# Another work order for a recurrent attention block: new TensorE orders and list priorities, masks and identity ahead of the first norm, W_O in sixteen loads

## The chip, the cores and the metric

The kernel runs on one core of one Trainium2 chip. The metric is the device time of one execution in microseconds (us). Before the change three runs gave 803.99, 806.18 and 807.5 us; the median is 806.18 us.

## The reference

```python
def _A_ref(x, mem0, Wq, Wk, Wv, Wo, seg_len):     # x 1 x 2048 x 512, 32 heads of 128, seg_len 32, M = 8
    mem = mem0
    for s in range(n_seg):                        # 64 segments
        xs = x[:, s * seg_len:(s + 1) * seg_len, :]
        h = jnp.concatenate([mem, xs], axis=1)    # 40 rows
        q, k, v = h Wq, h Wk, h Wv                # 512 -> 32 x 128 each
        scores = where(mask, q k^T * scale, -1e9)
        o = softmax(scores) v
        o = jnp.einsum('bhte,hed->btd', o, Wo)
        mem = o[:, :M, :]                         # the memory of the next segment
        outs.append(o[:, M:, :])
    return jnp.concatenate(outs, axis=1)

h = x + _A_ref(_layernorm(x), mem0, Wq, Wk, Wv, Wo, 32)
h2 = h + _B_ref(_layernorm(h), w1, b1, w2, b2)    # layernorm, 512 -> 1792, gelu, 1792 -> 512
```

What matters is the recurrence: the first eight output rows of a segment are the first eight input rows of the next one. All products are bf16 with sums in f32.

## The kernel before, in words

All of W_Q, W_K, W_V and W_O (4 MB each) are loaded once and stay on the chip. The segments then run one after the other. Of the 40 rows of a segment, 32 (8 of memory and the first 24 tokens) stand as columns in `hT`, and go through the Q, K and V passes (`passes`, lines 794 and 796; a *unit* is four to sixteen TensorE instructions, the smallest part that an order can name). The last 8 tokens of a segment influence no later segment. Those of four segments are put together in `hB` (one tile of 128 tokens) and their passes are *fill work*, called F0 and F1 in the orders: it is put where TensorE would otherwise wait for the recurrence. W_O of the gathered rows (`wo_B`, line 1112, reads `OTB`) is fill work of the fourth segment.

One segment on TensorE is: Q0, K0, Q1, K1 (two halves of the heads), the scores SC0 and SC1 (line 963), V0 and V1, PVA (line 1055, the 24 tokens of the segment before), PV0 and PV1 (lines 994 and 998, probabilities times values), WO (line 1083, eight units), SA (line 1025, scores of the tokens). Then the recurrence closes: VectorE transposes the product of WO (`TT`, line 1095) and adds its halves into the `hT` of the next segment (line 1089), and only then can the first pass of the next segment read it. Softmax runs on VectorE (maxima `nmc` 972, reciprocals `rsc` 979, products `PC` 982, transposes `PTC` 983) and ScalarE (exponentials `EC`, line 976). Copies of PSUM go to ScalarE or VectorE, as `either` decides (lines 814 and 815).

A Python class records every operation and sets the order of each engine before anything is built. TensorE's order is written by hand: `START` for the opening with segment 0, and one string of `ORDERS` for each *place*: a1 to a3 for the first segments, m0 to m3 for the four places of the repeating cycle (segments 4 to 59, 14 cycles), z60 to z63 for the last. In such a string `WO.0.2` means units 0 and 1 of WO. `TURNED` names the passes that run backward at a place, so that a pass can start on the weights that the one before left in the array (`matmul_kept`, line 547, a matmul without a weight load). `LOCK` and `LEAD` place extra weight loads that change nothing (line 794), so that a cycle has a whole number of blocks of 256 TensorE instructions. The other engines are list-scheduled: an operation is taken by its rank plus `BONUS[kind@place]`; `HOIST` lets a wait be taken by an earlier TensorE instruction.

The opening: GpSimd builds `maskA` (lines 689 and 690), `maskR` and `maskL` (661 to 687), then `OTB`'s own masks (884 and 887) and `ident` (656 and 657), and computes the inverse deviations of the first two tiles of x (`rst`, 736 and 737). VectorE clears `OT`, `ZC` and `KALL` (693 to 696), takes the statistics of those tiles (734 and 735) and normalizes them (`xn`, 738). TensorE transposes them (748). The weights are issued on the SyncE queue (708, then 719 to 722 for W_O in eight pieces of 512 KB), the first tiles of x, the first memory and the bias of the MLP on ScalarE's queue (`first`, 711). The tiles of x from the third on come later and are transposed by DMA (755). In the fourth place of a cycle the product of `wo_B` is copied and added (1118 and 1119), in the first place of the next cycle its halves are added (`oBn`, 1120), and in the second the tile is added to x (1130). After segment 63 the MLP closes the kernel.

## Time and profile before

| | |
|---|---|
| three runs | 803.99, 806.18, 807.5 us; median 806.18 us |
| the profiled execution | 803.95 us; its span 802.2 us |
| mean granted TensorE clock | 0.998 |
| busy: TensorE, VectorE, ScalarE, GpSimd | 97%, 75%, 70%, 11% of the span |
| moved in the first 50 us | 18.18 MB, mean 364 GB/s |

The page gives for each engine its busy time, for each group of instructions its count, mean duration and the idle time ahead of it, and names what ended that idle time. In answers with a time line each row has the start, the duration (of a row with x4: of the four together), the engine, the line and the tiles, and in brackets how long the engine had been idle and what released it. Matmuls overlap, so a row's duration reaches into the next row; what counts is the distance from start to start. The queues' rows are marked SPq and ACTq.

### The profile page before, as it was taken

How to read it: one execution, taken by the hardware profiler on the slowest of the kernel's cores; microseconds unless marked ns; L12 is line 12 of the kernel's file. 1: busy time of each engine (PE TensorE's matmuls, PEld its weight loads, DVE VectorE, ACT ScalarE, POOL GpSimd, SP SyncE). 2: the span in 40 equal slices, each digit the busy share in tenths (PEclk: the TensorE clock that was granted, in tenths of full speed). 3: DMA queues.
4: the chain of work that ended last, by engine and by line, in shares of the span. 5: the costliest groups of instructions: out<-in, count | busy, mean ns of one | idle time of the engine just before them, and what ended most of it. 6: DMA issues, size and time to landing. Idle time of an engine off the chain costs nothing.

```text
span 802.2 us, 46835 instructions
## 1 busy us (share of the span) xinstructions
PE 775.9 (97%) x21699; PEld 423.1 (53%) x20880; DVE 600.7 (75%) x1847; ACT 558.0 (70%) x1580; POOL 90.1 (11%) x211
## 2 busy tenths in 40 slices
PE   2899999999999999999999999999999999999998
PEld 1455555555555555555555555555555555644444
DVE  3277878888888888888888888888888888732311
ACT  1557777777777777777778777777777777773342
POOL 5022000010001010101010101000000000020700
PEclk9999999999999999999999999999999999999999
DMA  9961010201111121102010202010212112074300
GB/s 367 394 174 24 4 37 11 45 12 37 26 33 30 30 33 27 36 19 42 19 43 15 49 12 50 13 37 20 50 25 56 51 38 59 17 232 127 86 27 26
DMA packets 65555, 48.77 MB, mean 61 GB/s; under 512 B 28996, under 2 KB 63308, under 8 KB 63820
## 3 DMA queue, kind: packets, MB, share of 16 engines
q1 hardware_dynamic: 65024, 45.50, 20.3%
q8 instruction: 166, 2.72, 1.4%
q14 instruction: 33, 0.27, 0.1%
q10 hardware_dynamic: 332, 0.27, 0.1%
HBM read 31.08 MB, written 8.13 MB: 49 GB/s over the span
## 4 chain that ended last, share of the span: by engine, by line
PE 91%; DMA 3%; DVE 2%; ACT 1%; SPq 1%; issue 1%; POOL 0%; DVEq 0%; ACTq 0%
PE ps L796 43%; PE ps L1083 15%; PE ps L547 8%; PE quad L1465 6%; PE ps L1451 5%; DMA WQ<-in_A_Wq_dram 3%; PE ps L1112 3%; PE quad L994 3%; PE quad L1055 2%; PE ps L1025 2%; PE ps L1233 1%; PE ps L963 1%; PE quad L963 1%; SPq L708 1%; PE quad L998 1%
## 5 line engine op out<-in xcount | busy, mean ns | idle before, releaser
L1083 PE MATMUL ps<-WO,OT 128*32 128x256 bf16 x4224 | 140.6, 274 | 0.1
L796 PE MATMUL ps<-WQ,hT 128*32 128x512 bf16 x1864 | 131.6, 379 | 0.7 <-DVE hT L1089 0.5
L796 PE MATMUL ps<-WV,hT 128*32 128x512 bf16 x1364 | 125.2, 381 | 0.0
L796 PE MATMUL ps<-WK,hT 128*32 128x512 bf16 x1700 | 123.6, 380 | 0.1
L815 ACT ACTIVATE kq<-ps 128x512 bf16<-128x512 f32 x160 | 95.4, 597 | 32.3 <-PE ps L796 26.4
L1083 PEld LDWEIGHTS ps<-WO,OT 128*32 128x32 bf16 x4224 | 100.9, 96 | 26.5 <-ACT OT L814 5.5
L814 ACT CAST kq<-ps 128x512 bf16<-128x512 f32 x162 | 94.8, 585 | 19.9 <-PE ps L796 13.1
L814 ACT CAST OT<-quad 128x128 bf16<-128x128 f32 x191 | 84.4, 442 | 27.0 <-PE quad L998 18.8
L839 DVE STREAM_TRANSPOSE KALL<-kq 128x256 f32<-128x256 f32 x160 | 71.2, 445 | 15.0 <-ACT kq L814 11.8
L796 PEld LDWEIGHTS ps<-WQ,hT 128*32 128x32 bf16 x1864 | 50.3, 97 | 58.8 <-issue 19.0
L861 POOL COPY ZC<-QTB 128x256 bf16<-128x256 bf16 x64 | 25.6, 401 | 477.2 <-PE ps L963 455.7
L796 PEld LDWEIGHTS ps<-WK,hT 128*32 128x32 bf16 x1700 | 45.8, 96 | 56.9 <-issue 14.5
L547 PE MATMUL ps<-WV,hT 128*32 128x512 bf16 x684 | 67.6, 379 | 0.0
L796 PEld LDWEIGHTS ps<-WV,hT 128*32 128x32 bf16 x1364 | 38.4, 97 | 47.3 <-issue 36.6
L839 DVE STREAM_TRANSPOSE QT<-kq 128x256 f32<-128x256 f32 x128 | 57.0, 445 | 6.5 <-ACT kq L815 1.9
L1454 ACT ACTIVATE WQ<-ps,b1t 128x512 bf16<-128x512 f32 x42 | 28.9, 688 | 46.6 <-PE ps L1451 46.6
L1095 DVE STREAM_TRANSPOSE TT<-ps 128x256 f32<-128x256 f32 x66 | 29.7, 450 | 36.3 <-PE ps L1083 36.1
L814 ACT CAST VS<-ps 128x512 bf16<-128x512 f32 x65 | 38.1, 586 | 26.6 <-PE ps L796 26.5
L814 DVE CAST VS<-ps 128x512 bf16<-128x512 f32 x63 | 41.8, 663 | 5.4 <-PE ps L796 5.4
L1541 DVE TENSOR_TENSOR WV<-quad,WV 128x512 bf16<-128x512 f32 (+1 forms) x16 | 10.5, 672 | 45.6 <-PE quad L1465 45.6
L982 DVE TENSOR_TENSOR PC<-EC,rsc 128x128 bf16<-128x128 f32 x128 | 39.7, 310 | 4.3
L1112 PE MATMUL ps<-WO,OTB 128*32 128x512 bf16 x512 | 42.1, 381 | 0.4 <-issue 0.2
(163 smaller groups left out, 1432.1 us busy)
## 6 DMA issues: line engine op xcount, KB each, us to landing
WV<-in_A_Wv_dram SPq DMA_DIRECT2D x4, 1024.0 KB, 8.5
WK<-in_A_Wk_dram SPq DMA_DIRECT2D x4, 1024.0 KB, 14.2
WQ<-in_A_Wq_dram SPq DMA_DIRECT2D x4, 1024.0 KB, 24.7
WO<-in_A_Wo_dram SPq DMA_DIRECT2D x8, 512.0 KB, 9.4
v_last<-VSB SPq DMA_DIRECT2D x60, 64.0 KB, 2.9
VBD<-v_last SPq DMA_DIRECT2D x60, 64.0 KB, 2.9
h_mid<-xr SPq DMA_DIRECT2D x16, 128.0 KB, 1.8
WK<-in_B_w_dram SPq DMA_DIRECT2D x4, 512.0 KB, 4.6
```

Of the source, the lines that this page charges most:

```text
L547: return e.add_instruction(mybir.InstMatmult(name="I-%d" % (4000000 + _kept[0]), engine=mybir.EngineType.PE, start_tensor_calc=start, stop ...
L796: ins = e.matmul(o, l, m, start=(k == 0), stop=(k == DC - 1), tile_position=(0, 32 * j), skip_group_check=True)
L814: return {"act": (lambda e: e.copy(out, src), t_act(n, ps_)), "dve": (lambda e: e.tensor_copy(out, src), 0.16 + 1.042e-3 * n * fast)}
L815: return {"act": (lambda e: e.mul(out, src, scale_), t_act(n, ps_)), "dve": (lambda e: e.tensor_scalar(out, src, scale_, None, ALU.mult), ...
L839: S.op("dve", lambda e: e.transpose(out, src), reads=[("kq", i)], writes=[key], dur=t_dve(256) + 0.02, after=after)
L982: S.op("dve", lambda e: e.tensor_tensor(PC[:, r].rearrange("p t a -> p a t"), EC[:, r], bc, ALU.mult), reads=[("EC", r), ("rsc", r)], writ ...
L1083: ins = e.matmul(ps[bank][32 * j:32 * j + 32, 0:256], lhs(slot(h)), wo_cols(h, b), start=(k == 0), stop=(k == 15), tile_position=(0, 32 * ...
L1095: S.op("dve", lambda e: e.transpose(tt.rearrange("p c q t -> p (c q t)"), ps[bank][:, 0:256]), reads=[("ps", bank)], writes=[("TT", par)], ...
L1112: ins = e.matmul(ps[bank][32 * j:32 * j + 32, :], OTB[:, bk % 2, slot(h), :], WO[:, h, :], start=(k == 0), stop=(k == 7), tile_position=(0 ...
L1451: ins = e.matmul(ps[bank][:, 0:SBT], W1[:, cc, fc * P:(fc + 1) * P], hnT_of(k)[:, cc, :], start=(cc == 0), stop=(cc == DC - 1))
L1454: S.op("act", lambda e: e.activation(gT[:, fc, :], ps[bank][:, 0:SBT], ACTF.Gelu_apprx_tanh, bias=b1t[:, fc:fc + 1], scale=1.0), reads=[(" ...
L1465: S.op("pe", lambda e: e.matmul(quad[:, t, :], lhs, W2[:, fc, :], **flags), reads=[("W2", part_of(fc))] + gT_keys(k, fc), writes=[("ps", t ...
```

## The change

Nothing changes in what is computed. Four things change:

1. `BONUS`, the table of priorities, gets other numbers for all kinds and places; `TURNED`, `ORDERS`, `LOCK` (106 to 108) and `LEAD` (199 to 189) are replaced. `START`, the order of TensorE in the opening, is left as it is.
2. The priority of `ident` goes from -40 to 40, so that GpSimd builds it first, with the masks behind it.
3. The tiles 0 and 1 of x are issued first on ScalarE's queue, ahead of the memory `m0` and the bias `b1n`, and this order is fixed with `behind`.
4. W_O is loaded in 16 DMAs of two heads in place of 8 of four, and a unit of WO waits for the pieces that it reads.

```diff
-LOCK = 106
+LOCK = 108
...
-LATE, RAW, LEAD = 0, 12, 199
+LATE, RAW, LEAD = 0, 12, 189
...
-TURNED = {"a1": "K0 Q1 V0", "a2": "K0 Q0", "a3": "V1", "m0": "F0 F1 Q0 V0", "m1": "K0 K1 Q1 V0", ...
+TURNED = {"a1": "K1 Q0 Q1", "a2": "K0 K1 Q1 V0 V1", "a3": "Q0 V0", "m0": "F0 Q1 V0", "m1": "F0 K0 K1 Q1 V0", ...
...
-          "m3": "K0.0.1 Q0.0.2 ... SC1.0.1 F1.0.1 V1.3.4 PVA.0.2 PV0.0.1 F1.1.5 WO.0.1 PV1.0.1 WO.1.8 F1.5.7 SA.0.1 F1.7.8",
+          "m3": "K0.0.1 Q0.0.2 ... SC1.0.1 V1.3.4 F1.0.1 PVA.0.2 PV0.0.1 F1.1.4 WO.0.2 PV1.0.1 WO.2.8 F1.4.7 SA.0.1 F1.7.8",
...
         def first(fn, kb, writes):
-            S.dma(fn, kb, writes=writes, eng="act")
+            firsts.append(S.dma(fn, kb, writes=writes, eng="act", behind=firsts[-1] if firsts else None))
+        firsts = []
         load_x(0, first)
+        load_x(1, first)
         first(lambda e: e.dma_start(m0, A_mem0[0]), 8, ["m0"])
         first(lambda e: e.dma_start(b1n[:], b1_d), 4, ["b1n"])
-        load_x(1, first)
...
-        for g in range(4):
+        for q in range(8):
             for a in range(2):
-                h0 = 16 * (g // 2) + 8 * a + 4 * (g % 2)
-                load(lambda e, h0=h0: e.dma_start(WO[:, h0:h0 + 4, :], wo_d[:, h0:h0 + 4, :]), 590, [("WO", g, a)])
+                h0 = 16 * (q // 4) + 8 * a + 2 * (q % 4)
+                load(lambda e, h0=h0: e.dma_start(WO[:, h0:h0 + 2, :], wo_d[:, h0:h0 + 2, :]), 295, [("WO", q, a)])
...
-                S.op("pe", f, reads=[("WO", q // 2, a) for a in range(2)] + reads(q // 4), ...
+                S.op("pe", f, reads=[("WO", q, a) for a in range(2)] + reads(q // 4), ...
```

What stands where, at the three places of which the prediction speaks. From line 712 on, the lines of the changed kernel are one higher.

GpSimd in the opening, before. The two `rst` rows per tile of x end the norm's statistics:

```order
25 L666 AFFINE_SELECT maskL<-maskL 128x16
26 L884 MEMSET OTB 128x608
27 L887 AFFINE_SELECT OTB<-OTB 128x4x8 x4
28 L736 TENSOR_SCALAR rst<-agg 128x1
29 L737 TENSOR_TENSOR rst<-rst,cneg 128x1
30 L656 MEMSET ident 128x128
31 L657 AFFINE_SELECT ident<-ident 128x128
32 L736 TENSOR_SCALAR rst<-agg 128x1
33 L737 TENSOR_TENSOR rst<-rst,cneg 128x1
```

GpSimd at the same place of the changed kernel (`ident` is now at rows 6 and 9, ahead of all masks):

```order
27 L666 AFFINE_SELECT maskL<-maskL 128x16
28 L737 TENSOR_SCALAR rst<-agg 128x1
29 L738 TENSOR_TENSOR rst<-rst,cneg 128x1
30 L737 TENSOR_SCALAR rst<-agg 128x1
31 L738 TENSOR_TENSOR rst<-rst,cneg 128x1
32 L885 MEMSET OTB 128x608
33 L888 AFFINE_SELECT OTB<-OTB 128x4x8 x4
```

Both tiles' `rst` move ahead of the masks of `OTB`, and nothing of `ident` stands between them any more.

ScalarE later in the opening, in the softmax of segment 0, before (`EC` are the exponentials of the two halves in ps6 and ps7; `OT` takes the products PV0 and PV1; `maskAF` is put into a bank for SA):

```order
33 L976 ACTIVATE EC,smc<-ps6,nmc 128x64 x2
34 L976 ACTIVATE EC,smc<-ps7,nmc 128x64 x2
35 L815 ACTIVATE kq<-ps5 128x512
36 L814 CAST OT<-quad 128x4x4x8
37 L938 COPY ps5<-maskAF 128x256
38 L814 CAST OT<-quad 128x4x4x8
```

ScalarE at the same place of the changed kernel:

```order
32 L977 ACTIVATE EC,smc<-ps6,nmc 128x64 x2
33 L816 ACTIVATE kq<-ps5 128x512
34 L939 COPY ps5<-maskAF 128x256
35 L815 CAST OT<-quad 128x4x4x8
36 L977 ACTIVATE EC,smc<-ps7,nmc 128x64 x2
37 L815 CAST OT<-quad 128x4x4x8
```

The exponentials of the second half now stand behind a copy, a mask and the copy of PV0's product.

TensorE at the end of place m3, before (`WO,OTB` is the fill work, `WO,OT` the units of WO, `KALL,QT` is SA, `WQ,hT` the next segment's first pass):

```order
1221 L1112 MATMUL ps<-WO,OTB 32x512 x16
1222 L1083 MATMUL ps<-WO,OT 32x256 x8
1223 L994 MATMUL quad<-PTC,VS 128x16 x16
1224 L998 MATMUL quad<-PTC,VBD 128x64 x4
1225 L1083 MATMUL ps<-WO,OT 32x256 x56
1226 L1112 MATMUL ps<-WO,OTB 32x512 x8
1227 L1025 MATMUL ps<-KALL,QT 32x32 x32
1228 L1112 MATMUL ps<-WO,OTB 32x512 x4
1229 L796 MATMUL ps<-WQ,hT 32x512 x8
```

TensorE at the same place of the changed kernel:

```order
1265 L1113 MATMUL ps<-WO,OTB 32x512 x12
1266 L1084 MATMUL ps<-WO,OT 32x256 x16
1267 L995 MATMUL quad<-PTC,VS 128x16 x16
1268 L999 MATMUL quad<-PTC,VBD 128x64 x4
1269 L1084 MATMUL ps<-WO,OT 32x256 x48
1270 L1113 MATMUL ps<-WO,OTB 32x512 x12
1271 L1026 MATMUL ps<-KALL,QT 32x32 x32
1272 L1113 MATMUL ps<-WO,OTB 32x512 x4
1273 L797 MATMUL ps<-WQ,hT 32x512 x8
```

One unit of four matmuls of the fill work goes from ahead of WO to behind it.

VectorE at the end of place m0 in one of the 14 cycles, before:

```order
855 L1089 TENSOR_TENSOR opT<-TT 64x4x24 x2
856 L839 STREAM_TRANSPOSE KALL<-kq 128x256
857 L1120 TENSOR_TENSOR oBn<-OTB 32x512
858 L1095 STREAM_TRANSPOSE TT<-ps 128x256
859 L1089 TENSOR_TENSOR hT<-TT 64x4x8 x2
```

VectorE at the same place of the changed kernel:

```order
859 L1090 TENSOR_TENSOR opT<-TT 64x4x24 x2
860 L840 STREAM_TRANSPOSE KALL<-kq 128x256
861 L1121 TENSOR_TENSOR oBn<-OTB 32x512
862 L739 TENSOR_SCALAR xn<-xr,agg,rst 128x512
863 L1096 STREAM_TRANSPOSE TT<-ps 128x256
864 L1090 TENSOR_TENSOR hT<-TT 64x4x8 x2
```

The normalization of a later tile of x, which stood at the end of m3, has come between `oBn` and `TT`; it stands there in nine of the cycles.

## The prediction

> **What bounds the kernel now.** I read the page's totals first, then what ended the chain, then TensorE's waits.

> ```profile
> span 802.2 us, 46835 instructions
> PE 775.9 (97%) x21699; PEld 423.1 (53%) x20880; DVE 600.7 (75%) x1847; ACT 558.0 (70%) x1580; POOL 90.1 (11%) x211
> ...
> PE 91%; DMA 3%; DVE 2%; ACT 1%; SPq 1%; issue 1%; POOL 0%; DVEq 0%; ACTq 0%
> ```

> TensorE is busy for 97% of the span, and it is 91% of the chain that ended last. Its idle time is 802.2 - 775.9 = 26.3 us, and part of that is the opening, where nothing can run. A change of order that keeps all the work can win only from idle time or from a slower clock. So I looked up where TensorE waits, in the list of its waits (engine and line, what it waited for, total, times, longest).

> ```profile
> PE ps L924 <- POOL maskL L666: 9.3, 1, 9.3
> ...
> PE quad L748 <- DVE xn L738: 2.5, 1, 2.5
> ...
> PE ps L796 <- DMA WQ<-in_A_Wq_dram: 1.1, 1, 1.1
> ...
> PE ps L796 <- DVE hT L1089: 0.5, 2, 0.3
> ```

> The big waits are single ones, in the first 50 us. The wait on `hT`, the recurrence, is nearly absent: fill work covers it. The prediction therefore has two parts, the opening and the 14 cycles.

> **The opening: what the earlier norm is worth.** The first rows are GpSimd's and VectorE's, from the time line.

> ```profile
> 9.93 1.35 POOL L887 TENSOR_SCALAR_AFFINE_SELECT OTB<-OTB 128x32 bf16<-128x32 bf16 x4
> ...
> 12.57 0.29 POOL L657 TENSOR_SCALAR_AFFINE_SELECT ident<-ident 128x128 bf16<-128x128 bf16 x1
> ```

> ```profile
> 9.88 0.69 DVE L734 BATCH_NORM_STATS2 stt<-xr 128x6 f32<-128x512 bf16 x1 [6.82 <-DMA xr<-in_A_x_dram]
> ...
> 14.04 1.79 DVE L694 MEMSET KALL<- 128x2080 uint32 x1 [0.38 <-issue]
> ```

> The norm of tile 0 waits for the tile until 9.88, then on GpSimd for OTB's masks, which end at 11.28, and on VectorE `xn` stands behind a 1.79 us clear. In the changed kernel the tiles come first, the clears are done while the tile flies, and `rst` follows maskL directly. With `ident` (about half a microsecond) put ahead of masks that ended near 9.3, `rst` can run near 10 to 10.5 and TensorE can transpose near 11 to 12 in place of 16.04 (the first row below). What it does with that lead stands in TensorE's time line and in the chain.

> ```profile
> 16.04 0.61 PE L748 MATMUL quad<-ident,xn 128*128 128x128 bf16 x4 [2.50 <-DVE xn L738]
> 17.11 3.65 PE L796 MATMUL ps<-WV,hB 128*32 128x512 bf16 x32 [0.47 <-ACT hB L814]
> 20.51 2.61 PE L796 MATMUL ps<-WV,hT 128*32 128x512 bf16 x32
> ...
> 31.73 1.91 PE L796 MATMUL ps<-WK,hB 128*32 128x512 bf16 x32
> 33.47 0.82 PE L796 MATMUL ps<-WQ,hB 128*32 128x512 bf16 x12
> 35.34 0.40 PE L796 MATMUL ps<-WQ,hB 128*32 128x512 bf16 x4 [1.05 <-DMA WQ<-in_A_Wq_dram]
> ...
> 36.43 1.04 PE L796 MATMUL ps<-WQ,hB 128*32 128x512 bf16 x16
> 37.29 1.04 PE L796 MATMUL ps<-WQ,hT 128*32 128x512 bf16 x16
> 39.55 0.66 PE L963 MATMUL ps<-KALL,ZC 128*32 128x64 bf16 x32 [1.22 <-POOL ZC L861]
> ...
> 42.57 0.29 PE L994 MATMUL quad<-PTC,VS 32*128 32x16 bf16 x16 [0.44 <-ACT OT L814]
> ...
> 43.89 1.96 PE L796 MATMUL ps<-WQ,hB 128*32 128x512 bf16 x16
> ...
> 49.03 0.38 PE L796 MATMUL ps<-WQ,hT 128*32 128x512 bf16 x1
> ```

> ```profile
> 7.24 28.05 DMA WQ<-in_A_Wq_dram
> ```

> The chain goes through the last piece of W_Q, which lands at 7.24 + 28.05 = 35.29 us. The changed kernel moves the same bytes ahead of it, only the order of 260 KB changes. So TensorE still cannot finish the first Q pass before 35.3, however early it started. **The lead is worth nothing at its end**: the work from 17.11 to 33.47 ends some 3 us earlier (the first V pass must itself wait for W_V, so not the whole 4 to 5 us) and TensorE then waits some 5 us for W_Q in place of 1.05, with a unit here and there as the earlier pieces land. I take the gain at 0.

> **The opening: what it may cost.** The clock is the first cost. The table by stretches gives (busy times of PE, PEld, DVE, ACT and POOL, then the granted clock):

> ```profile
> 38.00:42.00 4.00, 1.98 (x76) 0.82 (x68) 2.40 (x9) 3.37 (x14) 1.14 (x3) 1.00 1.10 351
> 42.00:46.00 4.00, 3.56 (x113) 2.40 (x102) 1.98 (x6) 1.74 (x7) 0.00 (x0) 0.57 1.10 349
> ```

> A stretch that was half busy (1.98 of 4 us) is followed by one at a granted clock of 0.57, in which 16 matmuls took 1.96 us, against 1.04 at 36.43. The first V pass at 17.11, behind the long idle start, shows the same: 3.65 us for 32, against 1.91 at 31.73. In the changed kernel the new pause from about 30.5 to 35.3 is emptier than the stretch from 38 to 42, so I expect the three Q passes from 35.3 on (0.87 us each, start to start) to begin at half speed. In some 3.4 us, the length that fits the slow stretch of 42 to 46, half the work is done, a loss of 1.7 us. It reaches the scores, because SC at 39.55 waits for copies of these passes. Ends: 0, if the pause doesn't slow the clock, and 2.6, if all three passes run at half speed.

> [...]

> The second cost is ScalarE's new order. The rows before:

> ```profile
> 41.12 0.32 ACT L976 ACTIVATE EC<-ps,nmc 128x64 f32<-128x64 f32 x1
> ...
> 41.41 0.61 ACT L815 ACTIVATE kq<-ps 128x512 bf16<-128x512 f32 x1
> 42.19 0.27 ACT L814 CAST OT<-quad 128x128 bf16<-128x128 f32 x1 [0.16 <-PE quad L998]
> ```

> The last exponential started at 41.12 and PV1 followed at 42.57, 1.45 later. In the changed kernel the second half's exponentials wait behind the copy of PV0's product, which ends at 42.46, so the last one starts near 42.7 and PV1 near 44.2, 1.6 later. Some 0.3 of it comes back, since VectorE has less to do between. I take 1.3 (ends 0 and 1.6). Behind PV1 on TensorE stand SA and WO of segment 0, so it counts in full. [...] W_O in 16 pieces costs nothing that I can see: WO had no wait for a load, and the eight more issues lie on a queue that waits for the transfers anyway. Ends: 0 and 0.3. The opening in sum: 1.7 + 1.3 - 1.3 = **+1.7 us**, ends -1.3 and +4.5 (2.6 + 1.6 + 0.3).

> **The cycles: one more unit behind WO.** Rows at the end of an m2 and of the m3 behind it:

> ```profile
> 317.28 0.42 PE L1025 MATMUL ps<-KALL,QT 128*32 128x32 bf16 x32
> 317.53 1.06 PE L796 MATMUL ps<-WV,hB 128*32 128x512 bf16 x16
> 318.44 0.40 PE L796 MATMUL ps<-WK,hT 128*32 128x512 bf16 x4
> ...
> 327.70 0.60 PE L1112 MATMUL ps<-WO,OTB 128*32 128x512 bf16 x8
> ...
> 328.36 0.41 PE L1112 MATMUL ps<-WO,OTB 128*32 128x512 bf16 x4
> 328.86 1.26 PE L796 MATMUL ps<-WQ,hT 128*32 128x512 bf16 x20
> ```

> From the first fill behind WO to the first pass of the next segment it is 1.16 us at both (318.44 - 317.28, 328.86 - 327.70). This is the length of the recurrence, TT and the adds. In m2, SA and four units fill it. The 16 matmuls of the four take 0.91 (318.44 - 317.53), a unit of four 0.23. In m3 there are SA and three units, and the last one took 0.50 from start to start: 0.27 of waiting. The fourth unit behind WO, taken from ahead of it, uses this time. I take 0.20 a cycle, a little under a unit, 14 x 0.20 = **-2.8 us** (ends -3.8, all 0.27, and 0). The other places keep four units and SA behind WO in another order, all within 1.16: nothing.

> **The cycles: the norm between oBn and TT.** The same order stands once in the profile of before, and the other rows are the usual m0:

> ```profile
> 543.51 0.68 DVE L1120 TENSOR_TENSOR oBn<-OTB 32x512 bf16<-32x512 f32 x1
> 544.51 0.45 DVE L1095 STREAM_TRANSPOSE TT<-ps 128x256 f32<-128x256 f32 x1 [0.33 <-PE ps L1083]
> ```

> ```profile
> 584.68 0.68 DVE L1120 TENSOR_TENSOR oBn<-OTB 32x512 bf16<-32x512 f32 x1
> 585.46 0.41 DVE L1224 TENSOR_SCALAR xn<-xT,agg,rst 128x512 bf16<-128x512 bf16 x1
> 585.79 0.44 DVE L1095 STREAM_TRANSPOSE TT<-ps 128x256 f32<-128x256 f32 x1
> ```

> VectorE waits 0.33 us for WO ahead of TT. With the norm of 0.41 in it, TT starts 1.11 after oBn in place of 1.00, and the next segment starts later by as much: 9 x 0.10 = **+0.9 us** (ends 0 and 1.0). Kept matmuls and extra weight loads change in number, but weight loads overlap the matmuls and 16 units take the same step either way: 0, ends -0.8 and +0.8, because the pauses of TensorE that the list of waits doesn't explain may move.

> **The sum**: 1.7 - 2.8 + 0.9 = -0.2 us. Against the profiled execution that is 803.95 - 0.2 = 803.8; this execution lies 2.2 below the median of the runs shown, so against the median it is 806.18 - 0.2 = **806.0 us**. A measurement of this kernel can tell about 0.5%, 4.0 us: faster is under 802.1, slower over 810.2.

> **The rivals.** *The opening wins after all.* No slow clock behind the pause, none at 42 to 46 either, and PV1 hidden: -1.3 - 2.8 + 0.9 - 0.8 = -4.0, and without the norm's cost -4.9: 801.3 to 802.2, middle **801.8 us**. [...] Against it: the rows show PV1 bound by the exponentials.

> *The opening is cold.* All three Q passes at half speed, PV1 late by the whole 1.6, the slow stretch at WO as before, and only half of the m3 unit counts: 4.5 - 1.4 + 0.9 = +4.0, **810.2 us**, just at the bound; every further tenth makes it slower.

> *The recurrence gets longer* (this one ends slower). VectorE, 75% busy, has 0.33 us spare ahead of TT. If the new list puts more in front of it at other places (in m1 the add to x, line 1130, now stands directly ahead of TT, and copies of `ZC` go from ScalarE to VectorE), TT is late by 0.1 in each of the 56 segments: 5.6 in place of 0.9, so 1.7 - 2.8 + 5.6 = +4.5, **810.7 us**. It decides from 0.09 a segment on. Against it: VectorE also loses copies of `maskAF` to ScalarE at these places.

> *The change does nothing in the opening* and the cycles gain alone: -2.8 + 0.9 = -1.9, **804.3 us**.

> **How the numbers follow.** My forecast 806.0 has 0.40; the winning opening 0.25 (0.20 faster, 0.05 within); the cold opening 0.13 (0.09 slower, 0.04 within); the longer recurrence 0.14 (0.13 slower, 0.01 within); the neutral opening 0.08, all within 0.5%, of which it takes 0.05, with 0.03 for a slower case not named. Faster 0.20, within 0.55, slower 0.25. The range goes from 801.6, the winning opening, to 810.8, the longer recurrence.

> **What would show it.** In the changed profile: the transposes of tile 0 near 11 to 12 us; the wait for W_Q near 5 us ending at 35.3; a clock under 0.8 in the stretch behind it; PV1 over 1.5 us behind PV0; segment 1's first pass near 50.7 in place of 49.03; the last fill unit of m3 followed in 0.23 us; TT 1.11 behind oBn in nine cycles. I am wrong if W_Q lands earlier than 35, if the clock stays at 1.00 from 35 to 46, or if waits on `hT` appear in every segment.

## The result and the profile after

The changed kernel takes **810.01 us** (median of six runs, 809.52 to 810.27), and the kernel before 806.15 us in the runs beside it (six, 803.53 to 807.5). The ratio is 1.0058 with a 95% interval of 1.0038 to 1.0079: slower by 0.6%, 3.9 us. The forecast was 806.0. The profiled execution took 809.82 us with a span of 808.1 us, against 803.95 and 802.2 before; this pair differs by 5.9 us and not by 3.9, because the profiled execution of before is one of its faster ones. The accounts below are of the two profiled executions, so they have to add up to 5.9.

The page after, from the totals:

```profile
span 808.1 us, 46811 instructions
PE 778.0 (96%) x21683; PEld 421.0 (52%) x20865; DVE 589.9 (73%) x1849; ACT 558.4 (69%) x1578; POOL 87.4 (11%) x211
```

TensorE's idle time rose from 26.3 to 30.1 us, and its busy time by 2.1 us with the same work; its mean granted clock was 0.994 in this execution, against 0.998 before. The list of its waits (engine and line, what for, total, times, longest) has new rows:

```profile
PE ps L797 <- DMA WQ<-in_A_Wq_dram: 4.2, 2, 2.1
PE quad L995 <- DVE PTC L984: 2.8, 3, 2.2
...
PE ps L797 <- DMA WK<-in_A_Wk_dram: 1.0, 1, 1.0
PE ps L964 <- ACT ZC L854: 0.9, 1, 0.9
...
PE quad L1466 <- DVE WV L1542: 0.8, 2, 0.6
...
PE ps L1113 <- issue: 0.7, 2, 0.4
PE ps L797 <- DMA WV<-in_A_Wv_dram: 0.7, 1, 0.7
...
PE quad L749 <- DVE xn L739: 0.3, 1, 0.3
```

The wait for the norm fell from 2.5 to 0.3, as the change wants. The wait for W_Q rose from 1.1 to 4.2, and there are new waits for W_K and W_V (1.7 together), for the probabilities (PTC), for a copy of the queries (ZC), and in the MLP for a norm.

Where the 5.9 us lie is best read from the starts of TT, since one TT closes each segment. The two TT rows below are the last before and the last of the 14 cycles (segments 3 and 59), first of before, then after:

```profile
78.98 0.45 DVE L1095 STREAM_TRANSPOSE TT<-ps 128x256 f32<-128x256 f32 x1 [2.12 <-PE ps L1083]
...
657.92 0.45 DVE L1095 STREAM_TRANSPOSE TT<-ps 128x256 f32<-128x256 f32 x1 [2.16 <-PE ps L1083]
```

```profile
82.50 0.45 DVE L1096 STREAM_TRANSPOSE TT<-ps 128x256 f32<-128x256 f32 x1 [1.56 <-PE ps L1084]
...
662.57 0.45 DVE L1096 STREAM_TRANSPOSE TT<-ps 128x256 f32<-128x256 f32 x1 [1.96 <-PE ps L1084]
```

At segment 3 the changed kernel is 3.5 us late, at segment 59 4.65. The table has all parts, worked out from the starts of all TT rows and the ends of the spans:

| part | before | after | difference |
|---|---|---|---|
| start to TT of segment 0 | 47.97 | 51.96 | +4.0 |
| segments 1 to 3 | 31.01 | 30.54 | -0.5 |
| the 14 intervals that end with a TT of m0 | 144.94 | 149.63 | +4.7 |
| the same for m1 and m2 together | 287.22 | 287.26 | 0.0 |
| the same for m3 | 146.78 | 143.19 | -3.6 |
| segments 60 to 63 | 42.17 | 42.21 | 0.0 |
| TT of segment 63 to the end | 102.13 | 103.29 | +1.2 |

So there are three losses (the opening, m0 and the end) and one gain (m3).

**The opening.** TensorE's time line after; the rows of before that answer to these stand in the prediction:

```profile
10.76 0.61 PE L749 MATMUL quad<-ident,xn 128*128 128x128 bf16 x4 [0.33 <-DVE xn L739]
...
32.77 0.40 PE L797 MATMUL ps<-WQ,hB 128*32 128x512 bf16 x4 [2.09 <-DMA WQ<-in_A_Wq_dram]
35.30 0.62 PE L797 MATMUL ps<-WQ,hB 128*32 128x512 bf16 x4 [2.13 <-DMA WQ<-in_A_Wq_dram]
35.70 1.92 PE L797 MATMUL ps<-WQ,hT 128*32 128x512 bf16 x16
37.41 1.92 PE L797 MATMUL ps<-WQ,hB 128*32 128x512 bf16 x16
39.11 1.81 PE L797 MATMUL ps<-WQ,hT 128*32 128x512 bf16 x16
...
43.87 0.26 PE L995 MATMUL quad<-PTC,VS 32*128 32x16 bf16 x16 [0.26 <-DVE PTC L984]
...
46.33 0.26 PE L995 MATMUL quad<-PTC,VS 32*128 32x16 bf16 x16 [2.16 <-DVE PTC L984]
...
52.89 1.26 PE L797 MATMUL ps<-WQ,hT 128*32 128x512 bf16 x20
```

The norm is done 5.3 us earlier (10.76 against 16.04), W_Q lands at the same time (35.30 against 35.34), and what lies between is waiting. The Q passes then take 1.71 us from start to start in place of 0.87. PV1 comes 2.46 us behind PV0, where it was 0.76. The table by stretches (length, busy PE, PEld, DVE, ACT and POOL, then the granted clock, the DMA share and GB/s):

```profile
30.60:35.30 4.70, 0.47 (x9) 0.10 (x5) 0.45 (x1) 0.19 (x1) 0.00 (x0) 0.85 1.02 385
35.30:38.00 2.70, 2.70 (x28) 1.08 (x32) 0.45 (x1) 0.92 (x2) 0.00 (x0) 0.50 1.11 349
38.00:42.00 4.00, 3.23 (x48) 1.00 (x36) 1.97 (x5) 1.71 (x5) 0.74 (x2) 0.66 1.10 348
42.00:46.00 4.00, 1.48 (x52) 0.66 (x52) 2.08 (x9) 2.67 (x12) 0.40 (x1) 1.00 1.11 348
46.00:50.00 4.00, 3.67 (x112) 2.90 (x116) 2.57 (x8) 1.65 (x4) 0.00 (x0) 0.69 0.69 215
```

The clock was at half in the Q passes, as the prediction had it. Then came a second emptier stretch (1.48 of 4 us, the wait for PTC), and behind it a second slow one (0.69), in which W_O's units ran. The last term of the prediction's sum for the opening, -1.3 us, counted on the slow stretch of before (0.57 at 42 to 46) going away; a slow stretch was there all the same, 4 us later. The four runs below that keep this opening whole (4 to 7) have it too: clocks of 0.57, 0.65, 0.65 and 0.50 from 46 to 50 us.

**The cycles.** The end of m3 and the start of m0 in the same cycle, before and after. TensorE's rows:

```profile
286.42 0.86 PE L1112 MATMUL ps<-WO,OTB 128*32 128x512 bf16 x8
286.89 0.59 PE L1025 MATMUL ps<-KALL,QT 128*32 128x32 bf16 x32
287.31 0.41 PE L1112 MATMUL ps<-WO,OTB 128*32 128x512 bf16 x4
287.57 0.61 PE L796 MATMUL ps<-WQ,hT 128*32 128x512 bf16 x8
```

```profile
289.62 0.82 PE L1113 MATMUL ps<-WO,OTB 128*32 128x512 bf16 x11
290.84 0.38 PE L1113 MATMUL ps<-WO,OTB 128*32 128x512 bf16 x1 [0.40 <-issue]
...
291.25 0.41 PE L1113 MATMUL ps<-WO,OTB 128*32 128x512 bf16 x4
291.48 0.83 PE L797 MATMUL ps<-WQ,hT 128*32 128x512 bf16 x12
```

From the first fill to the next segment's first pass it was 1.15 us before, and is 1.86 now. In the changed kernel TensorE stops within a unit, between its 11th and 12th matmul, for 0.40 us and waits for nothing that the profile shows ("issue"). Before, a shorter stop of this kind lies in SA (0.42 from start to start, where 0.22 is usual), and costs nothing, since the recurrence needs 1.16 us anyway. With the fourth unit behind WO, no slack is left there. Over the 14 cycles the first pass after TT of m3 starts at the earliest 0.93 us behind it. Before, it is later than that in four cycles, by 0.7 us in all; as changed in ten, by 3.3 us.

The place is the end of a block of 256 instructions. This can be counted: take TensorE's records (matmuls, weight loads, waits) in order, and look for steps of more than 0.33 us from start to start within one unit, in segments 4 to 59. The 14 traces of this document (two here, twelve below) have 120 such steps, and the numbers of all 120 leave the same remainder when divided by 256.

So the 4.7 us of m0 have three parts. The stops before the first pass cost 2.6 us more than before (3.3 - 0.7). The norm ahead of TT costs 1.0, as the fifth run shows. The other 1.1 lie between the first pass and TT as well: 0.5 in the first m0, where TensorE waits for the probabilities, and some 0.05 in each of the others, and no run here shows their cause.

**The end.** SyncE's queue, first before, then after:

```profile
723.39 0.45 SPq L1178 DMA_DIRECT2D WQ<-h_mid  x1
...
724.37 2.68 SPq L1128 DMA_DIRECT2D oN<-oBn  x4
```

```profile
726.99 2.76 SPq L1129 DMA_DIRECT2D oN<-oBn  x3
729.92 0.35 SPq L1179 DMA_DIRECT2D WQ<-h_mid  x1
```

The second load of the MLP's input (`h_mid`) now stands behind three transfers of the last tile, and comes 6.5 us later (the segments are 4.7 us late by then). Its norm is what the MLP waits for in the list above (0.8 us).

### The profile page after: what moved, and what is told of

Same layout as the page of the kernel before. It is cut to its first block, busy times and chain, and to the rows that moved or that the text cites. A ratio compares the mean times of both kernels' runs of the same rounds, so it can differ in the third digit from the quotient of the medians.

```text
span 808.1 us, 46811 instructions
## 1 busy us (share of the span) xinstructions
PE 778.0 (96%) x21683; PEld 421.0 (52%) x20865; DVE 589.9 (73%) x1849; ACT 558.4 (69%) x1578; POOL 87.4 (11%) x211
## 4 chain that ended last, share of the span: by engine, by line
PE 90%; DMA 5%; SPq 2%; DVE 1%; issue 1%; ACT 0%; DVEq 0%
PE ps L797 43%; PE ps L1084 15%; PE ps L547 9%; PE quad L1466 4%; PE ps L1452 4%; PE ps L1113 4%; DMA WQ<-in_A_Wq_dram 3%; PE quad L995 3%; PE quad L1056 2%; PE ps L1026 2%; DMA WQ<-h_mid 1%; PE quad L964 1%; PE ps L964 1%; SPq L708 1%; PE quad L999 1%
## 5 line engine op out<-in xcount | busy, mean ns | idle before, releaser
L797 PE MATMUL ps<-WQ,hT 128*32 128x512 bf16 x1748 | 129.5, 384 | 0.9 <-DVE hT L1090 0.6
L797 PE MATMUL ps<-WK,hT 128*32 128x512 bf16 x1740 | 127.0, 379 | 0.1
L816 ACT ACTIVATE kq<-ps 128x512 bf16<-128x512 f32 x159 | 94.7, 596 | 30.1 <-PE ps L797 29.6
L815 ACT CAST kq<-ps 128x512 bf16<-128x512 f32 x162 | 94.7, 584 | 24.6 <-PE ps L797 17.6
L815 ACT CAST OT<-quad 128x128 bf16<-128x128 f32 x191 | 84.3, 441 | 27.1 <-PE quad L999 19.1
L797 PEld LDWEIGHTS ps<-WQ,hT 128*32 128x32 bf16 x1748 | 47.7, 97 | 57.4 <-issue 16.8
L797 PEld LDWEIGHTS ps<-WK,hT 128*32 128x32 bf16 x1740 | 48.2, 97 | 56.2 <-issue 19.8
L840 DVE STREAM_TRANSPOSE QT<-kq 128x256 f32<-128x256 f32 x128 | 56.2, 439 | 10.5 <-ACT kq L816 7.4
L815 ACT CAST VS<-ps 128x512 bf16<-128x512 f32 x65 | 38.0, 585 | 27.0 <-PE ps L797 26.9
L815 DVE CAST VS<-ps 128x512 bf16<-128x512 f32 x63 | 41.2, 654 | 6.6 <-PE ps L797 6.6
L1038 ACT ACTIVATE SA<-SA 128x256 f32<-128x256 f32 x64 | 26.7, 417 | 27.4 <-DVE SA L1037 26.1
L797 PE MATMUL ps<-WQ,hB 128*32 128x512 bf16 x512 | 39.1, 396 | 4.3 <-DMA WQ<-in_A_Wq_dram 4.2
```

What stands on the lines that cost most here:

```text
L797: ins = e.matmul(o, l, m, start=(k == 0), stop=(k == DC - 1), tile_position=(0, 32 * j), skip_group_check=True)
L815: return {"act": (lambda e: e.copy(out, src), t_act(n, ps_)), "dve": (lambda e: e.tensor_copy(out, src), 0.16 + 1.042e-3 * n * fast)}
L816: return {"act": (lambda e: e.mul(out, src, scale_), t_act(n, ps_)), "dve": (lambda e: e.tensor_scalar(out, src, scale_, None, ALU.mult), ...
L840: S.op("dve", lambda e: e.transpose(out, src), reads=[("kq", i)], writes=[key], dur=t_dve(256) + 0.02, after=after)
L1038: exps[:] = [S.named(S.op("act", lambda e: e.activation(SA[:], SA[:], ACTF.Exp), reads=["SA"], writes=["SA"], dur=t_act(256, False)), "SAe")]
```

## The experiments

All times are of runs beside the kernel before on the same chip; the ratio is to it. The kernel before took 806.46 us (median) beside runs 1 to 4, 806.89 beside 5 to 8 and 805.98 beside 9 to 12, so a difference of two medians from different sets is uncertain by up to 0.9 us from this alone. "TT" below is the start of TT of segment 0, which sums up the opening: 47.97 before, 51.96 as changed (50.79 to 52.59 in the five traces that have this opening whole). In the diffs, a line on `BONUS` sums up a longer list of numbers in words, and "..." marks what is left out.

**1. The old opening.** W_O stays in 16 pieces.

```diff
-        load_x(0, first)
-        load_x(1, first)
         first(lambda e: e.dma_start(m0, A_mem0[0]), 8, ["m0"])
         first(lambda e: e.dma_start(b1n[:], b1_d), 4, ["b1n"])
+        load_x(0, first)
+        load_x(1, first)
...
-BONUS["ident"] = 40, and the other unplaced kinds of the opening as changed
+BONUS["ident"] = -40, and the other unplaced kinds of the opening as before
```

> The changed kernel with the opening of before: the tiles of x behind the memory and the bias, ident behind the masks, and before's priorities for the kinds of the opening; W_O stays in 16 pieces, and all cycles stay as changed. Theory (the opening's order costs 4.0 us, by a cold clock and by the late exponentials): the first pass of segment 1 back near 49.0 us, time 810.0 - 4.0 = 806.0 us. Rival (the 16 pieces of W_O or their waits cost it): segment 1 stays near 53, time 810 us.

Measured: 806.18 us, ratio 0.9996 (0.998 to 1.0013), TT at 47.69 us. The order of the opening costs 3.8 us by the medians (5.0 by the ratios) and 4.3 us at TT, and W_O in 16 pieces nothing that shows.

**2. The pause filled.**

```diff
-         ("B", "Q", 0, (0, 5)), "Q0", ...
+         ("W", 7, 16), ("B", "Q", 0, (0, 5)), "Q0", ...
...
-LATE, RAW, LEAD = 0, 12, 189
+LATE, RAW, LEAD = 0, 12, 61
```

> The changed kernel with 16 units of the existing warm matmul (bank 7, 3.5 us at full clock) in TensorE's queue ahead of the first Q pass, and 128 fewer extra weight loads so that the blocks of 256 stay where they are. Theory (the pause before W_Q lands slows the clock): the three Q passes from 35.3 on take 0.87 us each again in place of 1.71, segment 1 starts about 2 us earlier, time 808.0 us. Rival (the clock does not matter, the opening is bound by the exponentials' place in ScalarE's queue alone): PV1 stays near 46.3 and the time near 810 us.

Measured: 807.97 us, ratio 1.0023 (1.0006 to 1.004), TT at 48.78. The clock was 1.00 from 30.6 to 42, the Q passes took 0.86 us each, and PV1 still came 2.1 us behind PV0 (43.62 and 41.51). The cold clock is real, and worth 2.0 us by the medians (2.8 by the ratios, whose intervals just touch), 3.2 us at TT. The clock then fell to 0.64 in 42 to 46.

**3. The old order of the exponentials.**

```diff
-BONUS["EC1"] = -31.53, and the unplaced kinds of the softmax as changed
+BONUS["EC1"] = -4.83, and the unplaced kinds of the softmax as before
```

> The changed kernel with before's priorities of the softmax kinds in the opening alone: the exponentials of the second half stand ahead of the mask and of PV0's copy again. Theory: PV1 follows PV0 by about 0.8 us in place of 2.46, segment 1 starts 1.7 us earlier, time 808.3 us. Rival (the cold clock is all of it): PV1 moves but WO of segment 0 then waits for something else, and the time stays at 810 us.

Measured: 807.31 us, ratio 1.0006 (0.9989 to 1.0024), TT at 48.03. PV1 follows PV0 by 0.75 us:

```profile
43.33 0.26 PE L995 MATMUL quad<-PTC,VS 32*128 32x16 bf16 x16 [0.63 <-DVE rsc L980]
...
44.08 0.27 PE L995 MATMUL quad<-PTC,VS 32*128 32x16 bf16 x16 [0.44 <-ACT OT L815]
```

The expectation for TT was 1.7 us, and it was 3.9. With PV1 early there was no second emptier stretch, and the clock stayed at 1.00 from 42 to 50. So one edit took away both its own wait and the slow stretch behind it, although the Q passes still began at half speed (0.50 at 35.3 to 38). That is one trace, against five with PV1 late and a clock of 0.50 to 0.69 from 46 to 50.

**4. The old tail.**

```diff
-BONUS["oNr"] = 40, no "hx", and the other unplaced kinds of the last transfers and the MLP as changed
+BONUS["oNr"] = -14.91, "hx" = -6.38, and the others as before
```

> The changed kernel with before's priorities for the kinds of the MLP and of the last transfers, so that the second load of h_mid stands ahead of the oN transfers on SyncE's queue again. Theory: the MLP's wait for the norm (0.8 us in the list of waits, near 736 us) goes, time 810.0 - 1.1 = 808.9 us. Rival (the end is late for another reason, in the last segments): no change, 810 us.

Measured: 809.88 us, ratio 1.0038 (1.0021 to 1.0056). The time doesn't tell it from the changed kernel. The trace does: the MLP's wait for the norm is gone from the list, and from the TT of segment 63 to the end it takes 102.58 us in place of 103.29. The other traces agree on the size: from the last TT to the end it takes 102.45 to 103.38 us in the eight with the changed tail (103.04 on average), and 102.12 to 102.58 in the six with before's (102.27). Shown: the cause of the wait, and 0.7 to 0.8 us in the traces. Not shown: a gain in the median.

**5. The norm out of m0.**

```diff
-                 reads=[("xr", tb % XR), ("ag", i), ("rs", i)], writes=[("xn", i)], dur=0.38)
+                 reads=[("xr", tb % XR), ("ag", i), ("rs", i)], writes=[("xn", i)], dur=0.75)
```

> The changed kernel with the planner's duration of the norm xn set to 0.75 in place of 0.38, so that the plan has it at the end of place m1 and no longer between oBn and TT of m0. Theory (the norm costs 0.1 a cycle where it stands): TT starts 1.01 behind oBn in all cycles in place of 1.12, the 14 intervals of m0 lose 1.0 us together, m1 stays at 10.22; time 809.0 us. Rival (m0 is longer for another reason alone): oBn to TT shrinks, but the intervals of m0 stay, 810 us.

Measured: 809.01 us, ratio 1.0029 (1.0008 to 1.0049). VectorE's rows at the end of an m0, as changed and in this run:

```profile
299.88 0.68 DVE L1121 TENSOR_TENSOR oBn<-OTB 32x512 bf16<-32x512 f32 x1
300.66 0.41 DVE L739 TENSOR_SCALAR xn<-xr,agg,rst 128x512 bf16<-128x512 bf16 x1
300.99 0.44 DVE L1096 STREAM_TRANSPOSE TT<-ps 128x256 f32<-128x256 f32 x1
```

```profile
297.57 0.68 DVE L1121 TENSOR_TENSOR oBn<-OTB 32x512 bf16<-32x512 f32 x1
298.58 0.45 DVE L1096 STREAM_TRANSPOSE TT<-ps 128x256 f32<-128x256 f32 x1 [0.33 <-PE ps L1084]
```

1.11 us became 1.01, as expected, and the median fell by 1.0 us (2.3 by the ratios, whose intervals overlap). In the trace the intervals of m0 lost 2.9 us: 1.0 between the next segment's first pass and TT (133.30 to 132.34 over the 14), which is the norm, and 1.9 ahead of that pass, which are fewer and shorter stops at the ends of blocks. These differ from one execution to the next, but not by chance alone: m0 and m3 together take 292.8 to 293.2 us in the six traces of the changed cycles with the norm there, and 290.8 to 291.3 in the four (5, 10, 11, 12) without it. Taking it out is worth some 2.0 us in the traces; 1.0 of it is explained, and why the stops shrink with it is open.

**6. The unit ahead of WO again.**

```diff
-F1.1.4 WO.0.2 PV1.0.1 WO.2.8 F1.4.7 SA.0.1 F1.7.8
+F1.1.5 WO.0.2 PV1.0.1 WO.2.8 F1.5.7 SA.0.1 F1.7.8
```

> The changed kernel with one unit of the fill work of m3 put ahead of WO again (F1.1.5 and F1.5.7 in place of F1.1.4 and F1.4.7), all else as changed. Theory (the unit behind WO takes the slack in which TensorE's pauses at the ends of blocks of 256 instructions were hidden): the 14 intervals of m3 grow by 2.9 us, those of m0 shrink by 2.0 to 2.5; time 810.0 + 0.6 = 810.6 us. Rival (the unit is a clean gain of 0.2 a cycle and m0 is long for another reason): m3 grows by 2.9, m0 stays, 812.9 us.

Measured: 811.8 us, ratio 1.0062 (1.0041 to 1.0083). The intervals of m3 grew by 4.0 us (147.17 against 143.19; one stop of 1.0 us among them), those of m0 shrank by 2.4 (147.25 against 149.63). The whole 2.4 lie ahead of the next segment's first pass, which is late in three cycles, by 0.9 us in all, where it was late in ten, by 3.3. That is the direction of the theory of the lost slack, and the rival's unchanged m0 is out. The share is not settled: the median rose by 1.8 us (0.3 by the ratios), between the 0.6 of the theory and the 2.9 of the rival, and in the traces of the fifth and eleventh run, with the unit still behind WO, the late passes sum to 1.4 and 1.0 us only.

**7. The blocks shifted.**

```diff
-LOCK = 108
+LOCK = 172
```

> The changed kernel with LOCK at 172 in place of 108: the ends of TensorE's blocks of 256 instructions fall 64 instructions earlier in every cycle, four of them in or behind the units of WO, where 256 instructions take some 2.0 us by the steps of the profile and not 2.5 to 3.1 as now. Theory (TensorE pauses where a block is used up faster than the next one arrives): more and longer pauses, some 0.5 us at three or four places of a cycle, at other places than now; time above 820 us. Rival (the pauses belong to the recurrence or to other transfers at the end of m3): they stay in m0 and m2, 810 us.

Measured: 817.58 us, ratio 1.0123 (1.0096 to 1.015). It is 7.6 us slower than the changed kernel (5.2 by the ratios), less than expected, but the stops moved where the ends of the blocks moved. The list of TensorE's waits has rows that the changed kernel lacks, in SA and within the units of WO:

```profile
PE ps L1026 <- issue: 1.5, 5, 0.3
...
PE ps L1084 <- issue: 0.7, 3, 0.3
```

The intervals of m1, m2 and m3 grew by 3.7, 2.8 and 3.6 us, and those of m0, where no block ends in the fill work any more, shrank by 3.2: the first pass starts 0.93 us behind TT in all 14 cycles. The rival is out: the stops belong to the blocks. That a stop comes of the next block's late arrival, the expectation's theory, is not shown by it. The expectation's 2.0 us for 256 instructions was too short, though: the 256 records ahead of the 22 stops in this trace took 3.0 to 4.3 us.

**8. The unit in the kernel before.**

```diff
-F1.1.5 WO.0.1 PV1.0.1 WO.1.8 F1.5.7 SA.0.1 F1.7.8
+F1.1.4 WO.0.2 PV1.0.1 WO.2.8 F1.4.7 SA.0.1 F1.7.8
```

> The kernel before with one edit: the end of m3 reads F1.1.4 WO.0.2 PV1.0.1 WO.2.8 F1.4.7 SA.0.1 F1.7.8 as in the changed kernel. By the prediction's step (14 times 0.20): 806.2 - 2.8 = 803.4 us. By the theory of the lost slack: m3 shrinks by 2.9 us, m0 grows by about 2 us because the pauses at the ends of the blocks are no longer covered; time about 805.3 us.

Measured: 813.07 us, ratio 1.0092 (1.0055 to 1.0128), and neither theory said so. The intervals of m3 shrank by 2.75 us, as both had it. Those of m0 grew by 9.7:

```profile
PE quad L994 <- DVE PTC L983: 4.8, 14, 0.4
...
PE ps L1112 <- issue: 2.3, 4, 1.0
...
PE ps L1083 <- DMA WO<-in_A_Wo_dram: 1.3, 1, 1.3
```

TensorE waits in nearly every m0 for the probabilities, 0.3 us each (before once in all), and VectorE's list of m0 stands in another order, since the planner laid it out anew. The stops at the ends of blocks are most of the rest: the first passes of m0 come 3.7 us later than before, in all. So this run doesn't price the unit alone.

The last row belongs to the opening, which is that of before. In this execution the stretch from 42 to 46 had a clock of 1.00, where it was 0.57, and TT came at 47.90, where it was 47.97: what the clock gave, TensorE spent in waiting for W_O.

```profile
42.00:46.00 4.00, 3.53 (x133) 2.55 (x128) 2.75 (x9) 2.13 (x6) 0.00 (x0) 1.00 1.10 348
```

**9. Both causes of the opening.** The edits of the second and the third run together.

```diff
+         ("W", 7, 16), ("B", "Q", 0, (0, 5)), "Q0", ...
...
+BONUS["EC1"] = -4.83, and the unplaced kinds of the softmax as before
```

> The changed kernel with both repairs of the opening at once: the 16 warm units in the pause before W_Q and before's order of the exponentials. The two alone brought segment 0 to its TT at 48.78 and 48.03 us, against 51.96 as changed. If the two costs add up, TT comes at 44.9 us. Theory (each repair alone also removes the second slow stretch of the clock, so they share it; what is left is bound by W_Q's landing at 35.3 and the softmax behind it): TT at 47.0 to 47.7 us, time 806.0 us. Rival (the warm units themselves cost time in the queue): TT later than 48.0.

Measured: 806.17 us, ratio 0.9996 (0.9983 to 1.0008), TT at 47.73. The two don't add up: 3.2 and 3.9 us alone, 4.2 together. The clock was 1.00 throughout, so the clock is not what is left. A row says what is:

```profile
47.27 0.40 PE L1084 MATMUL ps<-WO,OT 128*32 128x256 bf16 x8 [1.01 <-DMA WO<-in_A_Wo_dram]
```

The last piece of W_O lands near 47.2 us, and WO of segment 0 cannot end before it. The expectation had TT right and the bound wrong: it named W_Q and the softmax. The opening stands against its transfers twice, at W_Q and at W_O.

**10. The changed kernel repaired.** The first, the fourth and the fifth edit together: before's opening and tail, the norm out of m0, all orders of the cycles as changed.

```diff
+before's unplaced priorities and before's order of `first`
...
+writes=[("xn", i)], dur=0.75)
```

> The changed kernel with the cycles' orders as changed, but with before's opening (as in the first run), before's priorities of the tail, and the norm xn out of m0. The parts measured alone: opening -4.3 us, tail -0.7, norm -1.0 on the changed kernel's 810.0: 804.0 us, 2 us faster than before. Rival (the parts meet again in pauses at the ends of the blocks, which the cycles keep): 806 us, as before.

Measured: 804.16 us, ratio 0.9974 (0.9963 to 0.9984): faster than before by 0.26%, and as the sum of the parts had it. The opening and the tail are those of before here, so the gain is in the orders of the segments. Where in them the traces can't say: this profiled execution is only 0.6 us shorter than that of before (0.4 in segments 1 to 3, 0.4 in the cycles, the rest 0.2 longer), against 1.8 between the medians.

**11. Repaired, with the early opening kept warm.**

```diff
+         ("W", 7, 16), ("B", "Q", 0, (0, 5)), "Q0", ("B", "Q", 0, (1, 4)), "Q1", "Z", ("W", 5, 4), "SC0", ...
...
-LATE, RAW, LEAD = 0, 12, 189
+LATE, RAW, LEAD = 0, 12, 29
```

> The changed opening kept early, with the 16 warm units before W_Q, before's order of the exponentials, and four more warm units between the last Q pass and the scores, where TensorE waits 1.2 us in the profile of before; before's tail and the norm out of m0. Theory (the half busy stretch from 38 to 42 causes the slow stretch behind it): clock 1.00 from 42 to 46, TT of segment 0 at 46.5 us, time 802.8 us. Rival (four units are too few to keep the clock, or they delay the scores): TT at 47.5 or later, time 804 us.

Measured: 803.35 us, ratio 0.9963 (0.9948 to 0.9977), the fastest median of all, but with an interval that overlaps the tenth run's; TT at 47.57. The clock was 1.00 from 42 to 46 as the theory had it, but TT did not come to 46.5; TensorE waits 1.0 us for W_O here too.

**12. Repaired, with before's opening and four warm units.**

```diff
+         ... "Q1", "Z", ("W", 5, 4), "SC0", ...
...
-LATE, RAW, LEAD = 0, 12, 189
+LATE, RAW, LEAD = 0, 12, 157
```

> As the repaired kernel with before's opening, with only the four warm units between the last Q pass and the scores added. Theory: clock 1.00 from 42 to 46 where before had 0.57, TT of segment 0 at 46.5 us in place of 47.7, time 802.8 us. Rival: the units delay the scores by as much as they save, TT at 47.7, 804 us.

Measured: 804.08 us, ratio 0.998 (0.9968 to 0.9992), TT at 47.62. The stretch that answers to the 0.57 of before, here:

```profile
42.00:46.00 4.00, 3.56 (x137) 2.71 (x136) 2.76 (x9) 2.12 (x6) 0.00 (x0) 1.00 1.12 353
```

The clock is right and the gain isn't there: W_O binds. The eighth and the tenth run, without the four units, had 1.00 in this stretch as well, behind the same half busy stretch (1.99 of 4 us from 38 to 42). So whether a half busy stretch slows the clock is not set by the order alone, and these runs don't show that the four units did it.

## Why the prediction was wrong

The sign was missed: no change was forecast, -0.2 us as a sum, and the kernel became 3.9 us slower. The range held the time. The rival that came nearest was the cold opening, at 810.2 us. Step by step:

- **The gain of the early norm, taken at 0: right.** W_Q landed at 35.30, and the lead of 5.3 us was spent in waiting: by the list 3.1 us more for W_Q, and 1.7 for W_K and W_V.
- **The cold clock, 1.7 us: right in cause and size.** The three Q passes took 0.84 us more each in the first two, and the scores came 1.7 us later (41.24 against 39.55). The clock behind the pause was 0.50 (35.3 to 38), and the second run shows the cause by taking the pause away: 1.00 from 30.6 to 42. The half speed lasted some 5.4 us from 35.3 on (an estimate from the 0.50 over 2.7 us and the 0.66 over 4), where the prediction took the 3.4 of before's slow stretch.
- **The late exponentials, 1.3 us: right, mis-sized.** They cost 1.7 between PV0 and PV1 (2.46 against 0.76).
- **The last term of 1.7 + 1.3 - 1.3, the slow stretch of 42 to 46 going away: this step failed.** No run shows a gain of 1.3 us from it. It failed twice. First, there was nothing to return: the eighth and the tenth run have before's opening with a clock of 1.00 from 42 to 46, and TT at 47.90 and 47.99 us, where before had 0.57 and 47.97. The slow stretch was hidden behind W_O, for whose last piece TensorE waited until 47.2 and 47.5 us there, so the term is 0 and not 1.3. Second, the late PV1 made a new emptier stretch, and a slow one stood behind it in all five traces with this opening; in the third run, with PV1 in its place, it is gone. Without the return the term is 1.7 + 1.3 + 0 = 3.0, and with PV1's measured size 3.4, against the 4.0 measured. The costs were not independent terms, and the sum treated them so. Segment 1's first pass came at 52.89 us, where the prediction had 50.7.
- **The unit behind WO, 2.8 us: the mechanism was right in m3 (2.75 to 3.6 in the traces), and its price was left out.** The step said of the stops that the list of waits doesn't explain "0, ends -0.8 and +0.8". **This step failed too:** they were +2.6 us in m0, and another 1.1 us there has no shown cause. The 0.27 us that the prediction called "waiting" in m3 was also the cover of a stop at the end of a block. Rows of before showed such stops; the prediction knew them and didn't ask what covers them. The seventh run settles what the stops are: move the ends of the blocks, and the stops move. That the unit's place covers them rests on the sixth run and the rows at the end of m3: put the unit back, and m0 recovers 2.4 us, in one trace.
- **The norm between oBn and TT, 0.9 us: right for what it counted.** 1.0 by the fifth run. The stops grow with the norm by another 1.0 us in the traces, for a reason that is not shown.
- **The end, not in the sum at all: +1.2 us.** The prediction looked at SyncE's queue for W_O alone. The fourth run takes the wait away, with 0.7 us of it in the trace; in no median is it told apart.

The terms with their measured sizes: 4.0 - 0.5 + 4.7 - 3.6 + 1.2 = 5.8 us, for the profiled pair. Against the medians 3.9 us are to be explained. Executions of one kernel differ by a few us (the ten runs of the fourth kernel span 806.6 to 812.3), and the late first passes of m0 alone sum to anything between 1.0 and 3.5 us in the traces of the changed cycles, so the two profiles alone could not have given the size.

Open: how large a stop is at a given end, and why a cycle has it in one execution and not in the next. The seventh run cost 7.6 us where more than 10 were expected.

## What to carry to other kernels

An engine that starts earlier gains only up to the next transfer that it needs: here the norm was done 5.3 us earlier, and W_Q landed at 35.30 us, as before (35.34). If the engine idles until then, the work behind may be slower, as here at a clock of 0.50 behind a stretch that was busy for 0.47 of 4.70 us; look at where the last byte lands before moving anything ahead of it. Slack that looks like waste can be the cover of stops that no wait explains (here the late first passes of m0 sum to 3.3 us with the slack filled, and to 0.7 before), so ask what it hides before filling it. Terms that meet on one engine within a few microseconds (a cold clock, a late operand, the clock again) need not add up, and are better priced together: the two repairs of the opening gave 3.2 and 3.9 us alone, and 4.2 together.
